# Attention tail on the full tensor array, one more batch of u transposed by DMA, and a new order of work

## The chip, the cores and the metric

The kernel runs on one NeuronCore of a Trainium2 chip. The metric is the time of one execution on the device in microseconds. Five runs of the kernel before gave 216.16 to 217.98 us, with a median of 216.56 us. One execution was recorded by the hardware profiler; all durations below come from it.

The core has a tensor engine (PE), which multiplies matrices into PSUM and loads its stationary operand by separate instructions (PEld); a vector engine (DVE), a scalar engine (ACT) and a general engine (POOL); and SP, whose queue here issues most DMAs. Each engine takes its instructions in the order in which the program gives them, and waits on semaphores for the others.

## The reference

```python
# q, k, v: (8, 8, 576, 64); batch, heads, sequence, head size
kv  = np.einsum('bhsd,bhse->bhde', k, v)
out = np.einsum('bhsd,bhde->bhse', q, kv)
rms = np.sqrt(np.mean(out * out, axis=-1, keepdims=True) + 1e-06)
x   = out / rms * g_norm                     # heads joined: (8, 576, 512)

theta = x @ w_theta
zr, zi = x * np.cos(theta), x * np.sin(theta)
y = einsum('ts,bsd->btd', w_tok_r, zr) + einsum('ts,bsd->btd', w_tok_i, zi)
u = x + y
result = u + np.maximum(u @ w_ch, 0.0)       # float32
```

## The kernel before

**Tiling.** Each of the 8 batches has 576 rows: four full tiles of 128 rows (`NF` = 4, `P` = 128) and a tail of 64 (`T` = 64), five tiles in all (`NT`). The 512 channels are four pairs of heads (`HP` = 4), each of 128 channels. A tail is kept on all 128 partitions: its 64 rows stand there twice, so that the later stages can work on one half of the channels (or on sine and cosine) in each half of the partitions.

**Stages of a batch.** SP loads k, v and q. PE forms kv by head pair (`attention`, L641; tile kv), and ACT or DVE copy it as a block diagonal into `kv_bd` in half precision. q is cast (`qcast`) and transposed to `qT`, whose columns are rows of q: for batches 0 to 3 on PE (`turn_q_pair`, and `turn_q_tail` for the tail), for batches from `Q_DMA` = 4 on by two DMA transposes on SP's queue (`turn_q`, L625 and L631). `norm` (L678) makes raw = q times kv (PE, four matmuls for a full tile), its squares sq (ACT), their sums ss (DVE), the inverse root rt (POOL; ACT and DVE in batch 0) and x = raw times rt (DVE). `turn_x` transposes x on PE (xTps) and ACT copies it to xT with the gain. `phase` makes th = x w_theta (PE), then pt (ACT), f and fa (DVE), two Sin into tr (ACT) and z = x times sine and cosine (DVE). `mix` multiplies z by the turned mixers wT, nine matmuls for a sum y (PE), and DVE adds xT to make uT. `channel` multiplies uT by w_ch (PE, vps), and DVE finishes ot = max(vps, 0) + u, which SP stores.

**u in row order.** `channel` needs u itself, not turned. In batches 0 to 2 and in the last, PE transposes uT (ups, L1116) and ACT copies the outcome to u (L1132). In batches 3 to 6 (`U_FROM` = 3) the four full tiles are made by four DMA transposes on SP's queue instead (ub, L1154), one per 128 channels; the tail is still transposed by PE. There is one buffer for ub.

**The tail of raw.** For the tail, `qT` has 64 columns as the stationary operand, so each matmul fills half of the array's columns (the profile writes the form as 128*64). Two matmuls per head pair, one to each half of the partitions, make the two copies:

```python
for hp in range(HP):
    qT = st["qT", b][:, ti, hp, 0:P if ti < NF else T]
    for rows in (slice(0, P),) if ti < NF else (slice(0, T), slice(T, P)):
        nc.tensor.matmul(
            t[rows, hp * P:(hp + 1) * P], qT, kv_bd[b % 2][:, hp, :],
            start=(hp == 0), stop=(hp == HP - 1),
        )
```

The same half-wide form serves kv, and the tails of th, vps and ups.

**What sets the order.** Nothing is ordered by hand. Every piece of work is a task given to a planner (`Weave`): its name, the engines that can do it with a cost for each, a due time, its needs, and the buffers that it takes and frees. The due time is `START + PERIOD * b + first + every * i`, with (first, every) by stage from the table `DUE`. The planner walks through the tasks with its own clock and fixes the order of each engine's instructions, which engine does a copy, and when a buffer is used again. `SLACK`, `MARGIN`, `AHEAD`, `HOLD`, `DRAIN` and `ENTRY` weigh waits and changes of the array's form against due times. Where PE would have nothing to do before `WARM`, it is given idle work (`warm`, L394). So a change of one constant can move instructions on every engine. The time itself is the hardware's.

Of the kernel before, what the change touches and what calls it, by code (L numbers as in the profile page):

```python
# [15 lines left out]

PERIOD = 26.77
START = 4.0  # L20
DUE = {
    "load": (-21.61, 8.44),
    "theta": (0.63, 0),
    "mixers": (12.92, 0),
    "wch": (22.42, 1.25),
    "wT": (21.7, 1.67),
    ("phase", 0): (19.67, 0),
    ("mix", 0): (28.68, 4.96),
    ("channel", 0): (31.53, 7.53),
    ("phase", 1): (11.06, 3.64),  # L30
    ("mix", 1): (31.8, 5.24),
    ("channel", 1): (50.99, 10.37),
    ("first", 1): (-22.57, 1.61),
    "first": (0.46, 0),
    "cast": (27.66, 0.92),
    "turn_q": (-15.49, 0.49),
    "attention": (-2.51, 1.53),
    "norm": (-0.29, 4.11),
    "turn": (3.55, 1.73),
    "phase": (18.31, 3.76),  # L40
    "mix": (52.82, 3.62),
    "channel": (75.2, 4.08),
}
SLOTS = {
# [5 lines left out]
BANK = {"th": "mm", "y": "mm", "vp": "mm", "pu": "tp", "px": "tp"}  # L50
QUAD = 2
Q_DMA = 4
U_FROM = 3
X_FROM = 8
MIX_AFTER = 2
WCH_AFTER = 8
Q_SOFT = 0
QL_SOFT = 1

# [45 lines left out]
class Weave:  # L105
# [6 lines left out]


    SLACK = {"PE": 0.2, "ACT": 0.004, "DVE": 0.078, "POOL": 0.1, "SP": 0.05}
    MARGIN = {"PE": 0.247, "ACT": 0, "DVE": 0.537, "POOL": 0.1, "SP": 0.0}
    BEGIN = {"PE": 1.6, "ACT": 3.2, "DVE": 1.7, "POOL": 2.5, "SP": 0.73}
    WARM = 71.2
    COLD = 5.0
    URGENT = 5.5
    AHEAD = 0.27  # L120
    HOLD = 2.54
    DRAIN = 0.095
    ENTRY = {"F": 0.011, "R": 0.011, "H": 0.024, "K": 0.048, "Q": 0.048}
    ARRAY = {"F": 0, "R": 1, "H": 2, "K": 2, "Q": 3}
# [137 lines left out]
def kernel(  # L262
# [13 lines left out]
    nc = tc.nc  # L276
    B, H, S, D = q.shape
    C = H * D
    P = 128
    NF = S // P  # L280
    SF = NF * P
    T = S - SF
    NT = NF + 1
    SX = NT * P
    NK = C // P
    HP = H // 2
# [11 lines left out]
    weave = Weave(SLOTS)  # L298
# [6 lines left out]
    def ps(kind, shape, dtype, name):  # L305
        return psum.tile(shape, dtype, tag=kind, bufs=SLOTS[kind], name=name)
# [12 lines left out]
    kv_bd = []  # L319
    for i in range(2):  # L320
        t = const.tile([P, HP, P], FP16, tag=f"kvbd{i}", name=f"kvbd{i}")
# [11 lines left out]
    for i in range(2):  # L333
        t = const.tile([P, NT, H, D], FP16, tag=f"qcast{i}", name=f"qcast{i}")
        nc.gpsimd.memset(t[T:P, NF], 0.0)
        qcast.append(t)
    tails = []
    for i in range(2):
        kl = const.tile([P, H, D], FP32, tag=f"kl{i}", name=f"kl{i}")
        vl = const.tile([P, H, D], FP32, tag=f"vl{i}", name=f"vl{i}")  # L340
# [8 lines left out]
    wch = wpool.tile([P, NK, C], FP16, tag="wch", name="wch")  # L349
# [7 lines left out]
    st = {}  # L357

    def act(n, operands=0, small=False):
        cost = 0.1 + n / 1200.0 + 0.09 * operands  # L360
        return ("ACT", cost, cost + 0.14, False)

    def dve(cost, fast=False):
        return ("DVE", cost, cost + 0.14, fast)

    def pe(cost, form="F"):
        return ("PE", cost, cost + 0.22, form)

    def pool(n):
        return ("POOL", 0.12 + n / 1000.0, 0.17 + n / 1000.0, True)  # L370
# [269 lines left out]
                  uses=[f"qc{b}", f"qT{b}"], dma=dma(0.8))  # L640

    def attention(b, hp):
        def fn(e):
            if hp == 0:
                st["kv", b] = ps("kv", [P, HP, D], FP32, f"kv{b}")
            kvp = st["kv", b]
            for j in range(NT if b >= QUAD else NS):
                for r in range(2):
                    if b < QUAD:
                        half = slice(r * PH, (r + 1) * PH)  # L650
                        (kt, vt) = (st[kind, b, hp][half, j, :] for kind in "kv")
                    else:
                        (kt, vt) = (st[kind, b, hp][:, r, j, :] if j < NF
                                    else st[kind + "l", b][:, 2 * hp + r, :] for kind in "kv")
                    nc.tensor.matmul(  # L655
                        kvp[r * D:(r + 1) * D, hp, :], kt, vt,
                        start=(j == 0), stop=(j == (NT if b >= QUAD else NS) - 1),
                    )

        def keep(e):  # L660
            for r in range(2):
                src = st["kv", b][r * D:(r + 1) * D]
                dst = kv_bd[b % 2][r * D:(r + 1) * D, :, r * D:(r + 1) * D]
                if e == "ACT":
                    nc.scalar.copy(out=dst, in_=src)
                else:
                    nc.vector.tensor_copy(dst, src)

        weave.add(("kv", b, hp), [pe(0.58, "K") if b >= QUAD else pe(1.05, "Q")], due("attention" if b > 1 else "first", b, hp), fn,
                  needs=[("k", b, hp), ("v", b, hp)] + ([("kl", b), ("vl", b)] if b >= QUAD else []),  # L670
                  makes=[] if hp else [("kv", f"kv{b}")],
                  uses=[f"k{b}_{hp}", f"v{b}_{hp}"] + ([f"tails{b}"] if b >= QUAD else []) + ([f"kv{b}"] if hp else []))
        if b > 1 and hp == HP - 1:
            weave.add(("bd", b), [("ACT", 0.65, 0.8, False)], due("attention", b, hp) + 0.1, keep,
                      needs=[("kv", b, i) for i in range(HP)],
                      makes=[("bd", f"bd{b}")], uses=[f"kv{b}"])

    def norm(b, ti):  # L678
        raw, sq, ss, rt, x = (f"{n}{b}_{ti}" for n in ("raw", "sq", "ss", "rt", "x"))
        bank = "raw"  # L680
        at = due("norm", b, ti) if b > 1 else due("first", b, HP)

        def product(e):
            t = st[raw] = ps(bank, [P, C], FP32, raw)
            for hp in range(HP):
                qT = st["qT", b][:, ti, hp, 0:P if ti < NF else T]
                for rows in (slice(0, P),) if ti < NF else (slice(0, T), slice(T, P)):
                    nc.tensor.matmul(  # L688
                        t[rows, hp * P:(hp + 1) * P], qT, kv_bd[b % 2][:, hp, :],
                        start=(hp == 0), stop=(hp == HP - 1),  # L690
                    )

        def square(e):
            t = st[sq] = sb("sq", [P, C], FP32, sq)
            nc.scalar.activation(out=t[:], in_=st[raw][:], func=AFT.Square)  # L695

        def total(e):
            t = st[ss] = sb("ss", [P, H], FP32, ss)
            nc.vector.reduce_sum(  # L699
                out=t[:], in_=st[sq][:].rearrange("p (h e) -> p h e", h=H),  # L700
                axis=mybir.AxisListType.X,
            )

        def root(e):
            t = st[ss]
            nc.gpsimd.tensor_scalar(  # L706
                out=t[:], in0=t[:], scalar1=D * eps, scalar2=None, op0=ALU.add
            )
            r = st[rt] = sb("rt", [P, H], FP32, rt)
            nc.gpsimd.tensor_tensor(out=r[:], in0=t[:], in1=mhalf[:], op=ALU.pow)  # L710

        def root0(e):
            t = st[ss]
            nc.scalar.activation(out=t[:], in_=t[:], func=AFT.Sqrt, bias=eps_t[:])

        def invert0(e):
            r = st[rt] = sb("rt", [P, H], FP32, rt)
            nc.vector.reciprocal(r[:], st[ss][:])

        def scale(e):  # L720
            t = st[x] = sb("x", [P, C], FP16, x)
            nc.vector.tensor_tensor(  # L722
                out=t[:].rearrange("p (h e) -> p h e", h=H),
                in0=st[raw][:].rearrange("p (h e) -> p h e", h=H),
                in1=st[rt][:].unsqueeze(2).broadcast_to((P, H, D)),
                op=ALU.mult,
            )

        qTs = [("qT", b, i) for i in range(NT if b < Q_DMA else 2)]
        bds = [("bd", b)] if b > 1 else [("bd", b, hp) for hp in range(HP)]  # L730
        weave.add((raw,), [pe(0.226, "F" if ti < NF else "H")], at, product, needs=qTs + bds,
                  makes=[(bank, raw)], uses=[f"qT{b}", f"bd{b}"])
        weave.add((sq,), [act(C)], at, square, needs=[(raw,)], makes=[("sq", sq)], uses=[raw])
        weave.add((ss,), [dve(0.59)], at, total, needs=[(sq,)], makes=[("ss", ss)], uses=[sq])
        if b == 0:
            weave.add(("rt0", HP), [("ACT", 0.2, 0.35, False)], at, root0, needs=[(ss,)], uses=[ss])
            weave.add((rt,), [dve(0.12)], at, invert0, needs=[("rt0", HP)], makes=[("rt", rt)],
                      uses=[ss])
        else:
            weave.add((rt,), [("POOL", 2.0, 2.1, False)], at, root, needs=[(ss,)], makes=[("rt", rt)],  # L740
                      uses=[ss])
        weave.add((x,), [dve(0.6)], at, scale, needs=[(rt,)], makes=[("x", x)], uses=[raw, rt])
# [357 lines left out]
    def channel(b, ti):  # L1100
# [5 lines left out]

        pu_on = not U_FROM <= b < B - 1 or ti == NF

# [71 lines left out]
    def due(stage, b, i):  # L1180
        (first, every) = DUE.get((stage, b), DUE[stage])
        return START + PERIOD * b + first + every * i

# [59 lines left out]
```

## Time and profile before

| | us |
|---|---|
| median of five runs | 216.56 |
| the profiled execution, on the device | 217.98 |
| its span, first to last instruction | 216.2 |
| PE busy in the span | 204.2 |
| DVE busy | 178.0 |
| ACT busy | 150.0 |
| POOL busy | 86.5 |
| y on PE (L1067), 576 matmuls | 77.9 |
| th and vps of full tiles on PE (L971, L1125), 128 matmuls each | 31.7 each |
| raw of full tiles (L688), 96 matmuls | 8.6 |
| raw of tails (L688), 64 half-wide matmuls | 3.3 |
| ups of full tiles (L1116), 64 matmuls | 5.9 |
| u copies of full tiles on ACT (L1132), 16 | 9.1 |
| rt on POOL (L710), 31 | 53.9 |

Busy time of an engine is the time covered by its instructions. Consecutive matmuls overlap in the pipeline, so their durations sum to more than the time that they take one after another, and a busy PE can still be held up. The span is what the profiler saw; the time on the device has about 1.8 us around it. The granted clock of PE was full in every slice of the page. DMA moved 45.10 MB at 209 GB/s over the span, with the DMA engines busy most of the time until about 140 us and much less after it.

### The profile page before, as it was taken

What the parts mean: (1) busy time and instruction counts of PE and PEld (TensorE: products, weight loads), DVE (VectorE), ACT (ScalarE), POOL (GpSimd) and SP (SyncE); (2) the same over time, 40 slices, a digit from 0 to 9 for tenths busy, and PEclk for the clock granted to TensorE, in tenths of its full rate; (3) what the DMA queues carried; (4) which work ended last, traced back from release to release, by engine and by line L of the source; (5) the groups of instructions that cost most, each with busy time, mean ns of one, the idle gap of its engine ahead of it and who ended that gap; (6) DMA issues with size and microseconds to landing.
All of it is one profiled execution on the core that took longest, in us unless ns stands there. A gap on an engine that the chain in (4) does not pass through costs nothing.

```text
span 216.2 us, 5949 instructions
## 1 busy us (share of the span) xinstructions
PE 204.2 (94%) x2358; PEld 144.5 (67%) x2358; DVE 178.0 (82%) x357; ACT 150.0 (69%) x291; POOL 86.5 (40%) x101
## 2 busy tenths in 40 slices
PE   6799699999999999999999999999999999999992
PEld 4675377875768667867767677757685667577560
DVE  3295699778988999899999997999898999874652
ACT  2275599977894699978789877968697786740041
POOL 8040104874006740874286348525553645000000
PEclk9999999999999999999999999999999999999999
DMA  6999599999598599997999999784732251345524
GB/s 197 386 353 249 129 341 317 332 295 204 172 291 264 107 307 303 207 290 187 267 206 270 273 248 138 203 292 170 180 85 75 100 121 27 125 136 59 194 80 162
DMA packets 60287, 45.10 MB, mean 209 GB/s; under 512 B 31204, under 2 KB 53348, under 8 KB 60260
## 3 DMA queue, kind: packets, MB, share of 16 engines
q1 hardware_dynamic: 56096, 42.48, 69.8%
q0 software_dynamic: 4160, 2.25, 10.1%
q8 instruction: 18, 0.29, 0.6%
q14 instruction: 9, 0.07, 0.1%
q10 hardware_dynamic: 4, 0.00, 0.0%
HBM read 33.06 MB, written 9.44 MB: 197 GB/s over the span
## 4 chain that ended last, share of the span: by engine, by line
PE 57%; DVE 17%; DMA 12%; POOL 4%; issue 3%; SPq 3%; ACT 2%; DVEq 0%; ACTq 0%
PE y L1067 23%; PE vps L1125 11%; PE th L971 7%; DMA ql<-in_q_dram 6%; PE kv L655 6%; DMA v<-in_v_dram 5%; DVE f L987 3%; PE raw L688 3%; DVE ot L1136 3%; POOL rt L710 3%; PE xTps L918 2%; DVE uT L1078 2%; PE ups L1116 2%; DVE z L1024 2%; SPq L414 2%
## 5 line engine op out<-in xcount | busy, mean ns | idle before, releaser
L1067 PE MATMUL y<-wT,z 128*128 128x320 f16 (+1 forms) x576 | 77.9, 286 | 0.3 <-DVE ot L1136 0.3
L1067 PEld LDWEIGHTS <-z 128*128 128x128 f16 x576 | 54.5, 98 | 16.6 <-issue 2.1
L710 POOL TENSOR_TENSOR rt<-ss,mhalf 128x8 f32<-128x8 f32 x31 | 53.9, 1739 | 2.6
L706 POOL TENSOR_SCALAR ss<-ss 128x8 f32<-128x8 f32 x31 | 9.7, 314 | 67.0 <-DVE ss L699 66.4
L1125 PE MATMUL vps<-wch,uT 128*128 128x512 f16 (+1 forms) x192 | 36.5, 344 | 0.0
L1078 DVE SCALAR_TENSOR_TENSOR uT<-y,gcol,xT 128x320 f16<-128x320 f32 (+1 forms) x48 | 29.1, 612 | 6.3 <-PE y L1067 6.1
L983 ACT ACTIVATE pt<-th,magic_t 128x512 f32<-128x512 f32 (+1 forms) x40 | 25.6, 643 | 11.2 <-PE th L971 10.6
L971 PE MATMUL th<-wth,xT 128*128 128x512 f16 x128 | 31.7, 379 | 0.3 <-DVE f L987 0.2
L655 PE MATMUL kv<-v,k 128*64 128x64 f32 (+1 forms) x672 | 25.4, 222 | 1.5 <-DMA v<-in_v_dram 1.2
L987 DVE SCALAR_TENSOR_TENSOR f<-pt,th 128x512 f32<-128x512 f32 (+1 forms) x40 | 24.8, 626 | 2.1 <-ACT pt L983 2.1
L655 PEld LDWEIGHTS kv<-v,k 128*64 128x64 f32 (+1 forms) x672 | 22.6, 137 | 4.6 <-issue 2.7
L927 ACT ACTIVATE xT<-xTps,gcol 128x512 f16<-128x512 f16 (+1 forms) x32 | 20.1, 629 | 7.7 <-PE xTps L918 7.4
L1132 ACT COPY u<-ups 128x512 f16<-128x512 f16 (+1 forms) x24 | 12.1, 513 | 17.5 <-PE ups L1116 17.4
L1006 ACT ACTIVATE tr<-fa,pio_t 128x512 f16<-128x512 f32 x32 | 22.8, 719 | 2.0 <-DVE fa L994 1.9
L722 DVE TENSOR_TENSOR x<-raw,rt 128x512 f16<-128x512 f32 x32 | 21.9, 685 | 2.4 <-POOL rt L710 2.2
L699 DVE TENSOR_REDUCE ss<-sq 128x8 f32<-128x512 f32 x32 | 21.7, 679 | 2.1 <-ACT sq L695 1.7
L1006 ACT ACTIVATE tr<-f 128x512 f16<-128x512 f32 x32 | 20.0, 630 | 4.9 <-DVE f L987 4.7
L1125 PEld LDWEIGHTS <-uT 128*128 128x128 f16 (+1 forms) x192 | 14.8, 102 | 10.8 <-issue 0.5
L1024 DVE TENSOR_TENSOR z<-x,tr 128x1024 f16<-128x1024 f16 (+1 forms) x32 | 19.7, 619 | 1.1 <-ACT tr L1014 0.8
L971 PEld LDWEIGHTS <-xT 128*128 128x128 f16 x128 | 11.9, 98 | 11.7 <-ACT xT L927 0.9
L695 ACT ACTIVATE sq<-raw 128x512 f32<-128x512 f32 x32 | 18.8, 591 | 0.8 <-PE raw L688 0.8
L599 DVE CAST qcast<-q 128x512 f16<-128x512 f32 x32 | 13.4, 420 | 5.1 <-DMA q<-in_q_dram 5.1
(101 smaller groups left out, 261.9 us busy)
## 6 DMA issues: line engine op xcount, KB each, us to landing
q<-in_q_dram SPq DMA_DIRECT2D x32, 256.0 KB, 5.2
out_dram<-ot SPq DMA_DIRECT2D x32, 256.0 KB, 2.7
k<-in_k_dram SPq DMA_DIRECT2D x24, 256.0 KB, 5.2
v<-in_v_dram SPq DMA_DIRECT2D x24, 256.0 KB, 5.4
k<-in_k_dram SPq DMA_DIRECT2D x8, 288.0 KB, 5.6
v<-in_v_dram SPq DMA_DIRECT2D x8, 288.0 KB, 5.7
wst<-in_moe_w_theta_dram SPq DMA_DIRECT2D x4, 256.0 KB, 7.3
out_dram<-ot SPq DMA_DIRECT2D x16, 64.0 KB, 2.1
```

What stands on the lines that cost most here:

```text
L655: nc.tensor.matmul(kvp[r * D:(r + 1) * D, hp, :], kt, vt, start=(j == 0), stop=(j == (NT if b >= QUAD else NS) - 1),)
L699: nc.vector.reduce_sum(out=t[:], in_=st[sq][:].rearrange("p (h e) -> p h e", h=H), axis=mybir.AxisListType.X,)
L710: nc.gpsimd.tensor_tensor(out=r[:], in0=t[:], in1=mhalf[:], op=ALU.pow)
L722: nc.vector.tensor_tensor(out=t[:].rearrange("p (h e) -> p h e", h=H), in0=st[raw][:].rearrange("p (h e) -> p h e", h=H), in1=st[rt][:].un ...
L971: nc.tensor.matmul(t[:], xT[:, kc, :], wth[:, kc, :], start=(kc == 0), stop=(kc == NK - 1),)
L983: nc.scalar.activation(out=t[:], in_=st[th][:], func=AFT.Identity, bias=magic_t[:])
L987: nc.vector.scalar_tensor_tensor(out=t[:], in0=st[pt][:], scalar=MAGIC, in1=st[th][:], op0=ALU.subtract, op1=ALU.subtract,)
L1006: nc.scalar.activation(out=t[:, which, :], in_=src[:], func=AFT.Sin, scale=-RAD, bias=0.0 if bias is None else bias[:],)
L1024: nc.vector.tensor_tensor(out=t[:], in0=xb.unsqueeze(1).broadcast_to((P, w, C)), in1=st[tr][:, 0:w, :], op=ALU.mult,)
L1067: nc.tensor.matmul(st[y][:, c, :], z[:, kc * P:(kc + 1) * P], wT[m][:, cols], start=(c == 0 and m == 0) if open_sums else m == 0, stop=m = ...
L1078: nc.vector.scalar_tensor_tensor(out=st["uT", b][:, chunks, cols], in0=st[y][:], scalar=gcol[:], in1=st["xT", b][:, chunks, cols], op0=ALU ...
L1125: nc.tensor.matmul(t[half], uT(kc), wch[:, kc, r * n:(r + 1) * n], start=(kc == 0), stop=(kc == NK - 1),)
```

## The change

Three things change, and the constants of the planner with them.

1. The tail's 64 columns of `qT` are copied beside themselves (task `qTd`, on ACT, DVE or POOL as the planner chooses), so that the stationary operand has 128 columns, and raw of a tail is made by the same four full matmuls as a full tile. A full tile now needs only the full columns of `qT`; the tail needs the copy.
2. `U_FROM` goes from 3 to 2: the full tiles of u of batch 2 are made by four DMA transposes instead of 16 PE transposes and four ACT copies.
3. The due times and weights of the planner are new, so the order is planned anew on every engine. `attention` can now take several head pairs as one task (`KV_RUN`), but with `KV_RUN = 1` it takes one, as before.

```diff
-PERIOD = 26.77
+PERIOD = 26.95
...
-    "theta": (0.63, 0),
-    "mixers": (12.92, 0),
-    "wch": (22.42, 1.25),
+    "theta": (0.39, 0),
+    "mixers": (17.6, 0),
+    "wch": (24.7, 1.25),
...
-    ("mix", 1): (31.8, 5.24),
-    ("channel", 1): (50.99, 10.37),
-    ("first", 1): (-22.57, 1.61),
+    ("mix", 1): (31.68, 5.24),
+    ("channel", 1): (50.99, 7.88),
+    ("first", 1): (-24.56, 1.26),
...
-    "norm": (-0.29, 4.11),
-    "turn": (3.55, 1.73),
+    "norm": (-1.15, 4.11),
+    "turn": (4.17, 1.73),
...
-    "mix": (52.82, 3.62),
-    "channel": (75.2, 4.08),
+    "mix": (51.46, 2.87),
+    "channel": (75.2, 4.3),
...
-U_FROM = 3
+U_FROM = 2
...
-    MARGIN = {"PE": 0.247, "ACT": 0, "DVE": 0.537, "POOL": 0.1, "SP": 0.0}
+    MARGIN = {"PE": 0.247, "ACT": 0.026, "DVE": 0.555, "POOL": 0.1, "SP": 0.0}
...
-    WARM = 71.2
+    WARM = 69.7
...
-    AHEAD = 0.27
-    HOLD = 2.54
+    AHEAD = 0.3
+    HOLD = 2.45
...
             for hp in range(HP):
-                qT = st["qT", b][:, ti, hp, 0:P if ti < NF else T]
-                for rows in (slice(0, P),) if ti < NF else (slice(0, T), slice(T, P)):
-                    nc.tensor.matmul(
-                        t[rows, hp * P:(hp + 1) * P], qT, kv_bd[b % 2][:, hp, :],
-                        start=(hp == 0), stop=(hp == HP - 1),
-                    )
+                nc.tensor.matmul(
+                    t[:, hp * P:(hp + 1) * P], st["qT", b][:, ti, hp, :], kv_bd[b % 2][:, hp, :],
+                    start=(hp == 0), stop=(hp == HP - 1),
+                )
...
-        qTs = [("qT", b, i) for i in range(NT if b < Q_DMA else 2)]
+        qTs = [("qT", b, i) for i in range(HP)] if b < Q_DMA else [("qT", b, 0)]
+        if ti == NF:
+            qTs.append(("qTd", b))
+
+            def double(e):
+                (out, src) = (st["qT", b][:, NF, :, r * T:(r + 1) * T] for r in (1, 0))
+                if e == "ACT":
+                    nc.scalar.copy(out=out, in_=src)
+                elif e == "DVE":
+                    nc.vector.tensor_copy(out, src)
+                else:
+                    nc.gpsimd.tensor_copy(out, src)
+
+            weave.add(("qTd", b), [act(HP * T), dve(0.2, True), pool(HP * T)], at - 1.0, double,
+                      needs=[("qT", b, HP if b < Q_DMA else 1)], uses=[f"qT{b}"])
...
-        weave.add((raw,), [pe(0.226, "F" if ti < NF else "H")], at, product, needs=qTs + bds,
+        weave.add((raw,), [pe(0.226)], at, product, needs=qTs + bds,
                   makes=[(bank, raw)], uses=[f"qT{b}", f"bd{b}"])
```

In the planned order this gives 5 doubling copies on ACT and 3 on POOL, 32 full matmuls for raw of the tails instead of 64 half-wide ones, 16 ups matmuls fewer, four DMA transposes more on SP's queue, and 50 pieces of idle work on PE instead of 55.

More of the change, by code (lines that the diff above doesn't have):

```diff
@@ L56 @@
 WCH_AFTER = 8
+KV_RUN = 1
 Q_SOFT = 0
@@ L642, in attention, with times @@
     def attention(b, hp):
+        run = KV_RUN if b >= QUAD and b > 1 else 1
         def fn(e):
-            if hp == 0:
+            if hp == run - 1:
                 st["kv", b] = ps("kv", [P, HP, D], FP32, f"kv{b}")
+            for i in range(hp - run + 1, hp + 1):
+                times(i)
+        def times(hp):
             kvp = st["kv", b]
@@ L667, in keep @@
                     nc.vector.tensor_copy(dst, src)
[L669 to L672, printed above, removed]
+        if hp % run == run - 1:
+            pairs = range(hp - run + 1, hp + 1)
+            kvn = [("kv", f"kv{b}")]
+            weave.add(("kv", b, hp), [pe(0.58 * run, "K") if b >= QUAD else pe(1.05, "Q")],
+                      due("attention" if b > 1 else "first", b, hp), fn,
+                      needs=[(kind, b, i) for kind in "kv" for i in pairs]
+                      + ([("kl", b), ("vl", b)] if b >= QUAD else []),
+                      makes=kvn if hp == run - 1 else [],
+                      uses=[f"{kind}{b}_{i}" for kind in "kv" for i in pairs]
+                      + ([f"tails{b}"] if b >= QUAD else []) + ([] if hp == run - 1 else [f"kv{b}"]))
         if b > 1 and hp == HP - 1:
             weave.add(("bd", b), [("ACT", 0.65, 0.8, False)], due("attention", b, hp) + 0.1, keep,
-                      needs=[("kv", b, i) for i in range(HP)],
+                      needs=[("kv", b, i) for i in range(run - 1, HP, run)],
                       makes=[("bd", f"bd{b}")], uses=[f"kv{b}"])
```

## The prediction

> **What bounds the kernel now.** I read first the page's totals and its row of 40 slices, then busy time by stretches of 20 us, then the order of time on the tensor engine (PE).
>
> ```profile
> PE 204.2 (94%) x2358; PEld 144.5 (67%) x2358; DVE 178.0 (82%) x357; ACT 150.0 (69%) x291; POOL 86.5 (40%) x101
> PE   6799699999999999999999999999999999999992
> PE 57%; DVE 17%; DMA 12%; POOL 4%; issue 3%; SPq 3%; ACT 2%; DVEq 0%; ACTq 0%
> ...
> 80.00:100.00 20.00, 20.00 (x288) 15.03 (x286) 18.88 (x37) 18.12 (x36) 9.94 (x11) 1.00 1.06 255
> 100.00:120.00 20.00, 20.00 (x223) 14.29 (x222) 19.15 (x39) 16.77 (x33) 10.30 (x10) 1.00 0.98 240
> 120.00:140.00 20.00, 19.87 (x245) 14.88 (x244) 18.67 (x37) 15.79 (x31) 11.58 (x13) 1.00 1.22 213
> 140.00:160.00 20.00, 20.00 (x235) 14.14 (x234) 18.87 (x38) 15.02 (x28) 9.45 (x9) 1.00 0.68 195
> ```
>
> The columns of the stretches are the span, then PE, weight loads, DVE, ACT and POOL. From 80 to 160 us PE has no gap and DVE is busy 75.6 of 80. But a busy PE may still be waiting inside a pipelined matmul, so what counts is the distance from one start to the next:
>
> ```profile
> 75.20 0.39 PE L918 MATMUL xTps<-ident,x 128*128 128x128 f16 x4
> 75.52 0.41 PE L688 MATMUL raw<-kvbd,qT 128*64 128x128 f16 x8
> 75.77 0.63 PE L655 MATMUL kv<-v,k 128*64 128x64 f32 x16
> 76.24 0.28 PE L655 MATMUL kv<-vl,kl 128*64 128x64 f32 x4
> 76.35 0.34 PE L655 MATMUL kv<-v,k 128*64 128x64 f32 x6
> ...
> 110.22 0.40 PE L918 MATMUL xTps<-ident,x 128*128 128x128 f16 x4
> 110.45 0.39 PE L688 MATMUL raw<-kvbd,qT 128*128 128x128 f16 x4
> 110.68 0.39 PE L1116 MATMUL ups<-ident,uT 128*128 128x128 f16 x4
> 110.90 0.38 PE L1125 MATMUL vps<-wch,uT 128*128 128x512 f16 x1
> ```
>
> Each row is one group: start, duration, tile written, array form. Groups of one kind have the same distance to their successor nearly everywhere after 62 us: four 128x128 pieces 0.23, four of 128x512 0.86, nine of 128x320 1.22. The few longer ones in the rows to 190 us add up to about 1.8 us of real waiting. **So from 62 us to the end the sum of PE's pieces sets the time**, and DVE is close behind. Loads are not near: between the landing of a batch's last k or v and its first use lie 5 us or more from batch 2 on.
>
> **Part 1, the tail's product.** It goes from eight pieces in the half-wide form (128*64) to four full ones. The rows price it: 75.52 to 75.77 is 0.25; 110.45 to 110.68 is 0.23, and 0.22 elsewhere. Eight batches by 0.03: **−0.24**. What speaks against the change is a rule of the Trainium skill: TensorEngine Tiling (Array Packing), Overview, gives up to twice the speed for a stationary operand of at most 64 columns, packed in tiles. But here both halves compute the same rows twice, so two packed pieces do what one doubled piece does, and the row shows no gain left to lose: read as a factor of two lost the rule would give +0.25 per batch, +2.0 in all; the row gives −0.24, and I take the row.
>
> The same page (Tiling Modes, Key Properties) says that a change of tiling mode drains the engine. The row agrees and gives the size: xTps takes 0.32 before the half-wide product and 0.23 before a full one, so 0.10 per change of form. If every tail shed its two changes, that would be 16 x 0.10 = 1.6 us. I counted the changes in both orders instead: 61 before, 57 after, because the tail mostly stood beside kv pieces, which are half-wide too, and keep their own changes. **−0.40.** I take the count.
>
> **Part 2, the doubling copies.** Eight of 128x256 f16: five on ACT, three on POOL. No row shows this one; the nearest are ACT's u copy of 128x256 (372 ns, L1132) and POOL's copy into wtt of 128x256 (399 ns, L528). So ACT +1.9, POOL +1.2. From below a copy can't cost less than nothing; from above it delays the raw of the tail by about 0.4 + 0.3 of handover, eight times. The cover: the transposed q's tail lands long before use (batch 4 at 100.1 us against its raw at 116.2, batch 5 at 121.3 against 136.8), and in the new order full tiles no longer wait for the tail's columns. On POOL only rt and ss are queued behind it, and POOL is 40% busy; on ACT, Sin and Square wait 0.37. I take 0 of PE's time, up to 0.8 if the cover on ACT is gone in some batches.
>
> **Part 3, u of batch 2.** Off PE: 4 groups of four transposes, 4 x 0.22 = **−0.88**. Off ACT: 4 x 0.584 (L1132) = −2.3. Added: four DMA transposes issued by SP, each 1.24 us of SP's queue, 2.5 us to landing in the quiet stretches and up to 4.8 in the crowded one. They go between the loads of batch 6 and the q transposes of batch 5, so SP's queue shifts by 5 us; behind it are k and v of batch 6, which landed 10.6 to 19.6 us before use. The finishing adds of batch 2 (DVE, in order) wait for the landing: from the last y of batch 2 to its first product with w_ch the new order has about 15 us of PE pieces at the rows' prices, against 11 for the adding of uT (0.55), the issue of a q transpose that stands before the last one (4.3, L625), its own 1.24 and 4.8 to landing. No cost at PE; if that cover failed, DVE would stop us for us.
>
> **Part 4, the new order.** The other gap it can close stands at 61 us, where PE has nothing ready while ACT copies kv of batch 2 (L665):
>
> ```profile
> 61.12 0.73 ACT L665 CAST kvbd<-kv 64x256 f16<-64x256 f32 x2
> 61.24 0.27 PE L394 MATMUL warm<-kvbd 128*128 128x256 f16 x1
> 61.35 0.28 PE L891 MATMUL qTpl<-ident,qcast 128*128 128x64 f16 x4
> 61.47 0.38 PE L394 MATMUL warm<-kvbd 128*128 128x256 f16 x2
> 62.15 0.38 PE L688 MATMUL raw<-kvbd,qT 128*128 128x128 f16 x4
> ...
> 64.29 0.45 DVE L1024 TENSOR_TENSOR z<-x,tr 128x512 f16<-128x512 f16 x1
> 64.77 0.49 PE L1067 MATMUL y<-wT,z 128*128 128x256 f16 x3
> ```
>
> The idle-work pieces (warm) fill 0.11 + 0.68 = 0.79 us. In the new order ups and vps of batch 0 stand there, and one idle piece follows later: 0.79 − 0.11 = **−0.68**. But the last rows show a second thin place. y of a batch can't start before z of its tail, which comes from th of the tail through pt, f, fa, two Sin and z. In the old order batch 1's z ended at 64.74 and y began at 64.77, with nothing to spare. Chain from th's start to z's end, against the PE pieces between th's start and y in the new order, priced by the rows: batch 1 6.66 against 5.96; batch 3 6.66 against 6.36; batch 7 4.72 against 4.30; the others are covered by 1 us or more. If the chains stay as long, PE waits 0.70 + 0.30 + 0.42 = 1.42. They may shorten (in batch 7 f waited 0.7 for DVE), so between 0 and 1.4: I take half, **+0.7**, since in the old order a chain could be slow unpunished. The sum over the other small waits I leave as it is, ±1 us. Before 40 us nearly all instructions keep their places: 0, ±0.4.
>
> **Sum:** −0.24 − 0.40 − 0.88 − 0.68 + 0.7 = −1.5. The profiled execution took 217.98 (span 216.2 and 1.8 around it) and would take 216.5; the median shown, 216.56, is 1.4 below the profiled one, and I carry the difference over: **215.1**, own range 213.8 to 216.2.
>
> **Rivals.**
>
> *Forecast: faster by PE's sum (0.54).* For it: the even distances between starts. Time 215.1.
>
> *No change: DVE takes over (0.23).* DVE has only 4.4 us free between 80 and 160 and gives back little: its list of copies loses some 0.8 us (three more of about 0.4 to 0.45, six fewer, at the rows' durations), nearly all in the first 75. If DVE holds the pace from 62 to 160, what PE saves there (0.88 of u, 5 x 0.03 of tails, about 0.3 of form changes: 1.3) comes back as waits, and 0.2 is left: 216.4. Against it: PE shows no waits there, so DVE runs ahead.
>
> *Slower: the tail's chain is uncovered (0.23).* Place: the head of each batch's y, in batches 1, 3 and 7 first. Price: the full shortfall is 1.42; each us by which ACT or DVE stretch a chain (copies put in, another order of f, x, ot) adds up to 1 us per such batch. Savings without waits are 2.2, so it decides from 2.2 + 1.1 = 3.3 us of new waits, that is chains longer by 0.6 us in three batches. At 1 us longer: 1.42 + 3.0 − 2.2 = +2.2, or 218.8; at 0.7, 217.9. For it: fillers became thinner in exactly these batches while DVE is nearly full; against it: ACT has lost 2.3 us at batch 2, and the chains had slack in the old order except at batch 1.
>
> That the change doesn't do what it says is excluded for parts 1 to 3: in the new order 64 half-wide pieces have become 32 full ones, 16 transposing matmuls are gone and four DMA transposes have come.
>
> **Numbers.** A measurement of this kernel can tell about 0.5% (1.1 us) from no change: faster is below 215.5, slower above 217.6. The forecast's own spread puts about 0.52 below 215.5 with a little from better orders; the second case and the forecast's upper end give 0.25; the third 0.23. The range goes from 213.3 (no shortfall, other waits 1 less) to 218.0 (third case at 0.7).
>
> **What would show it.** Right: rows of raw with x4 in the full form for tails, 0.22 apart; no ups of batch 2; starts as even as now after 62 us; no idle pieces near 61; y of batch 1 starting within 0.5 us after the pieces before it. Wrong: waits of PE's y for DVE's z of the tail in batches 1, 3 or 7; waits of DVE's ot for the DMA ub; waits of ACT for the landing of qT's tail; DVE at 20.0 of 20 in the stretches with PE waiting for it.

## The result, and the profile after

The changed kernel takes 214.56 us (median of 24 runs, 213.75 to 217.62) against 216.51 us for the kernel before (45 runs): a ratio of 0.9914, 95% interval 0.9898 to 0.9930, or 1.9 us less. Medians are of all runs; ratios leave out the few runs in a slower state. The forecast was 215.1, with a range of 213.3 to 218.0. The profiled execution of after took 216.28 us with a span of 214.5; that of before 217.98 with 216.2. They lie 1.7 and 1.5 above their medians, so the two spans may be compared.

First the page of after: totals, and the shares of the chain that ended last.

```profile
PE 203.8 (95%) x2305; PEld 144.9 (68%) x2305; DVE 177.2 (83%) x355; ACT 150.6 (70%) x294; POOL 89.0 (41%) x104
PE 58%; DMA 15%; DVE 8%; ACT 7%; POOL 6%; issue 2%; SPq 2%; DVEq 0%
```

PE has 53 matmuls fewer and DVE, ACT and POOL have nearly the same work. In the chain, DVE's share fell from 17% to 8%, and DMA's rose from 12% to 15%. Next the stretches of 20 us (span, PE, weight loads, DVE, ACT, POOL, then granted clock and DMA):

```profile
80.00:100.00 20.00, 19.77 (x252) 14.21 (x247) 19.57 (x41) 18.83 (x39) 10.14 (x11) 1.00 1.06 254
100.00:120.00 20.00, 20.00 (x235) 15.05 (x233) 19.46 (x39) 17.23 (x32) 11.63 (x13) 1.00 0.87 203
120.00:140.00 20.00, 20.00 (x237) 14.64 (x235) 18.96 (x37) 15.00 (x30) 10.14 (x10) 1.00 0.95 240
140.00:160.00 20.00, 20.00 (x229) 13.44 (x226) 19.89 (x39) 16.28 (x32) 12.95 (x12) 1.00 0.76 220
```

PE is still full, but DVE now works 77.9 of these 80 us, where it worked 75.6 before. Its total hardly changed (177.2 for 178.0), but more of it falls into this stretch, and 2.1 us are left free.

To see where the time went I took the distance from each group's start on PE to the next start, and subtracted the price that the same pieces have where nothing holds them up. What is left is idle work, waits and changes of form:

| us | before | after |
|---|---|---|
| pieces at their undisturbed price | 181.5 | 180.4 |
| rest, before 40 us | 18.9 | 18.4 |
| rest, 40 to 70 us | 2.6 | 3.0 |
| rest, 70 to 190 us | 6.6 | 6.4 |
| rest, from 190 us | 0.8 | 0.8 |

The pieces' own sum gives 1.1 of the 1.5 that this account shows, as parts 1 and 3 said; the other 0.2 between the spans lies behind PE's last piece. The 0.5 before 40 us says nothing, since executions of one order stand up to 2.5 us apart there (last section). The rest hides gains and losses that nearly cancel, and they are in the rows in order of time. The tail's product of batch 2, in the full form, among its neighbours:

```profile
76.14 0.39 PE L943 MATMUL xTps<-ident,x 128*128 128x128 f16 x4
76.36 0.39 PE L699 MATMUL raw<-kvbd,qT 128*128 128x128 f16 x4
76.58 0.39 PE L1141 MATMUL ups<-ident,uT 128*128 128x128 f16 x4
```

Starts are 0.22 apart, as forecast. At 61 us the idle pieces are gone. One stands at the head of y of batch 1:

```profile
65.75 0.28 PE L395 MATMUL warm<-kvbd 128*128 128x256 f16 x1
66.09 4.09 PE L1092 MATMUL y<-wT,z 128*128 128x256 f16 x36
```

Elsewhere such a piece takes 0.11 to the next start (61.24 to 61.35 in before). Here it takes 0.34: y starts just behind its end, at 65.75 + 0.28 = 66.03. This looks like the wait for z of the tail that the prediction named, at half its size, for DVE makes that z at about the same time (square brackets give the engine's idle time before the row, and what ended it):

```profile
65.57 0.43 DVE L1049 TENSOR_TENSOR z<-x,tr 128x512 f16<-128x512 f16 x1 [0.22 <-ACT tr L1039]
```

It ends at 66.00. But it is not that wait. In `d2_dve_more` (below) DVE is a little later against PE; the distance is 0.34 again, and y starts 0.11 before z has ended:

```profile
65.25 0.28 PE L395 MATMUL warm<-kvbd 128*128 128x256 f16 x1
65.59 4.09 PE L1093 MATMUL y<-wT,z 128*128 128x256 f16 x36
```

```profile
65.27 0.43 DVE L1050 TENSOR_TENSOR z<-x,tr 128x512 f16<-128x512 f16 x1 [0.23 <-ACT tr L1040]
```

In all eight profiles of kernels with after's order here, the distance is 0.33 or 0.34. And in after, y of batch 2 starts at 93.99 (rows below), when z of its tail is only being begun:

```profile
94.00 0.42 DVE L1049 TENSOR_TENSOR z<-x,tr 128x512 f16<-128x512 f16 x1 [0.43 <-ACT tr L1039]
```

In batch 3, y starts at 111.62 and z of the tail ends at 111.80; neither y is held up. The kernel says why: a sum y is nine matmuls, and only the ninth (`m == 2 * NF`) reads z of the tail. At 0.11 each, that is 0.87 us after y's start, and in every batch from 1 on z was ready by then, in after with 0.4 us or more to spare. So the 0.34 is the price of the idle piece itself.

In batch 7 the prediction named a shortfall of 0.42, and there is none. y follows the pieces before it at once:

```profile
192.32 0.68 PE L1150 MATMUL vps<-wch,uT 128*64 128x256 f16 x8
192.93 4.24 PE L1092 MATMUL y<-wT,z 128*128 128x256 f16 x37
```

Two waits are new and had not been named. In the first, PE stops for DVE's x behind y of batch 2:

```profile
93.99 2.13 PE L1092 MATMUL y<-wT,z 128*128 128x256 f16 x18
96.35 0.40 PE L943 MATMUL xTps<-ident,x 128*128 128x128 f16 x4 [0.23 <-DVE x L733]
```

From 93.99 to 96.35 are 2.36 us for eighteen pieces that take 1.97 elsewhere. DVE had itself waited 0.43 for the Sin in front of z of the tail (row at 94.00), and x is the fourth piece behind that z in its queue. So the tail's chain probably does cost time here, through DVE's order and not through y; no run separates this. The second is the larger one. The first product with w_ch stops in the middle for its weights:

```profile
54.51 0.60 PE L1150 MATMUL vps<-wch,uT 128*128 128x512 f16 x2
55.80 0.59 PE L1150 MATMUL vps<-wch,uT 128*128 128x512 f16 x2 [0.69 <-DMA wch<-in_moe_w_ch_dram]
56.23 0.39 PE L783 MATMUL qTps2h<-ident,qcast 128*128 128x128 f16 x4
```

From 54.51 to 56.23 are 1.72 us for a group that takes 0.86. POOL's queue in the same execution shows why:

```profile
43.85 1.68 POOL L855 TENSOR_TENSOR rt1h<-ss1h,mhalf 128x8 f32<-128x8 f32 x1
45.50 1.51 POOL L544 DMA_DIRECT2D wch<-in_moe_w_ch_dram  x2
```

Its two fetches stand behind one more root task than before. The new due time of w_ch (24.7 for 22.42) is not what put them there: with the old due times and the edits (`c1_old_constants`, below) they stand behind the same third root and are issued at 44.8, and with the new due times alone (`c2_constants_alone`) they stand in front of it and are issued at 40.8. So they moved with the edits, by way of the planner. They were issued at 41.7 and 42.4 before and are issued at 45.5 and 46.3 now; their landing takes 8.2 to 9.5 us, and PE wants the second 8.6 us after its issue.

### The profile page after: what moved, and what is told of

It is laid out like the page before. It is cut to its first block, busy times and chain, and to the rows that moved or that the text cites. A ratio compares the mean times of both kernels' runs of the same rounds, so it can differ in the third digit from the quotient of the medians.

```text
span 214.5 us, 5833 instructions
## 1 busy us (share of the span) xinstructions
PE 203.8 (95%) x2305; PEld 144.9 (68%) x2305; DVE 177.2 (83%) x355; ACT 150.6 (70%) x294; POOL 89.0 (41%) x104
## 4 chain that ended last, share of the span: by engine, by line
PE 58%; DMA 15%; DVE 8%; ACT 7%; POOL 6%; issue 2%; SPq 2%; DVEq 0%
PE y L1092 25%; PE vps L1150 12%; PE th L996 8%; DMA ql<-in_q_dram 6%; PE kv L662 5%; DMA wch<-in_moe_w_ch_dram 4%; POOL rt L721 3%; DMA v<-in_v_dram 3%; PE raw L699 2%; PE xTps L943 2%; POOL rt1h L855 2%; ACT tr L1031 2%; DMA k<-in_k_dram 2%; PE ups L1141 2%; DVE x L733 2%
## 5 line engine op out<-in xcount | busy, mean ns | idle before, releaser
L721 POOL TENSOR_TENSOR rt<-ss,mhalf 128x8 f32<-128x8 f32 x31 | 55.8, 1801 | 2.6
L717 POOL TENSOR_SCALAR ss<-ss 128x8 f32<-128x8 f32 x31 | 8.4, 272 | 56.6 <-DVE ss L710 55.9
L662 PE MATMUL kv<-v,k 128*64 128x64 f32 (+1 forms) x672 | 27.0, 233 | 0.0
L662 PEld LDWEIGHTS kv<-v,k 128*64 128x64 f32 (+1 forms) x672 | 24.2, 146 | 3.7 <-issue 3.1
L1157 ACT COPY u<-ups 128x512 f16<-128x512 f16 (+1 forms) x20 | 9.9, 500 | 16.8 <-PE ups L1141 16.8
```

Source lines behind the costliest of these rows:

```text
L662: nc.tensor.matmul(kvp[r * D:(r + 1) * D, hp, :], kt, vt, start=(j == 0), stop=(j == (NT if b >= QUAD else NS) - 1),)
```

## The experiments

Twelve more kernels ran, each 5 to 22 times, with the kernel before beside it. Ratios are to before; differences between kernels are taken between ratios, times 216.5 us, since the median of before moved from 216.5 to 216.8 between sets.

**Undoing one part in the new order.** In these the planned order of everything else is exactly that of after.

`a1_half_wide`: the tail's product half-wide again, without the copies.

```diff
-                nc.tensor.matmul(
-                    t[:, hp * P:(hp + 1) * P], st["qT", b][:, ti, hp, :], kv_bd[b % 2][:, hp, :],
+                qT = st["qT", b][:, ti, hp, 0:P if ti < NF else T]
+                for rows in (slice(0, P),) if ti < NF else (slice(0, T), slice(T, P)):
+                    nc.tensor.matmul(
+                        t[rows, hp * P:(hp + 1) * P], qT, kv_bd[b % 2][:, hp, :],
...
```

> The order of the changed kernel, but raw of each tail again from eight half-wide matmuls, and no doubling copies. By the sum of PE's pieces: 8 x 0.03 for the pieces, and the changes of the array's form rise from 57 to 71, 14 x 0.10, together +1.6 us: 216.2 against 214.6 of the changed kernel. If DVE sets the pace: 0 to +0.3, 214.6 to 214.9. If the copies cost time where they stand: less than +1.6 by what they cost.

Measured: 215.51, ratio 0.9951 (0.9933 to 0.9970), so 0.8 us above after. The same tail of batch 2 here:

```profile
73.81 0.39 PE L947 MATMUL xTps<-ident,x 128*128 128x128 f16 x4
74.12 0.41 PE L701 MATMUL raw<-kvbd,qT 128*64 128x128 f16 x8
74.47 0.40 PE L1145 MATMUL ups<-ident,uT 128*128 128x128 f16 x4
```

The distances are 0.31 and 0.35, where after has 0.22 and 0.22: two changes of form and eight pieces cost 0.22 more. That holds for the tails of batches 2, 4, 5 and 6; in batch 3 a wait of 0.1 hides part of it, and in batch 7 the tail follows a half-wide vps, and raw and its neighbours take 2.52 us in both. The sum over batches 2 to 7 is 1.0. The expected 1.6 counted all eight tails at full price, the first two of which lie in the front.

`a4_half_copies`: the same, with the copies kept.

```diff
 half-wide product as in a1_half_wide; the task qTd copies as in after
```

> The order of after with the half-wide tail again and the doubling copies kept, though nothing reads what they write. Against a1_half_wide (215.5), which differs by the copies alone, the copies cost nothing if the work beside them hides them: 215.5. If they delay ACT or POOL, up to the 0.8 that the prediction allowed: 216.3.

Measured: 215.68, ratio 0.9970 (0.9939 to 1.0000). That is 0.4 us above a1, with intervals that overlap. In the profile the distance between the two grows by 0.2 us from 27 us to the end, and 0.14 of this is a longer wait for w_ch at 53 us. The copies are hidden, or nearly so.

`a2_u_by_pe`: u of batch 2 by PE and ACT again, in front of its products with w_ch, and its four DMA transposes left out.

```diff
+            if b == 2 and ti < NF:
+                turn(e)
+                nc.scalar.copy(out=st["ub", b][:, ti, :], in_=st[pu][:])
             t = st[vp] = ps(BANK["vp"], [P, n], FP32, vp)
...
```

> The order of the changed kernel, but u of batch 2 again from PE transposes and ACT copies, each put just ahead of the tile's product with w_ch; its four DMA transposes left out. By the sum of PE's pieces: 4 x 0.22 = +0.9 us, 215.5; a little more if the four ACT copies (2.3 us) delay a Sin that PE waits for. If DVE sets the pace: +0 to +0.2.

Measured: 215.25, ratio 0.9951 (0.9928 to 0.9975), 0.8 above after. In its order of time each ups takes the place that it was priced at:

```profile
120.08 0.39 PE L1141 MATMUL ups<-ident,uT 128*128 128x128 f16 x4
120.30 1.03 PE L1153 MATMUL vps<-wch,uT 128*128 128x512 f16 x4
121.17 0.39 PE L1141 MATMUL ups<-ident,uT 128*128 128x128 f16 x4
```

Four times 0.22 is lost there and nowhere else. Part 3's price stands.

`a3_wch_early`: the two fetches of w_ch, and the hold in front of them, moved up in POOL's queue before the second of its root tasks of batch 1; nothing else moves.

```diff
...
+        early = [x for x in log if x[0] in ("hold_ch", ("wch", 0), ("wch", 1))]
+        log = [x for x in log if x not in early]
+        at = [x[0] for x in log].index(("rt1h1",))
+        for (_, e, fn) in log[:at] + early + log[at:]:
+            fn(e)
```

> The order of the changed kernel, but the two fetches of w_ch stand earlier in POOL's queue, before the second root of batch 1, so that the first product with w_ch no longer waits for them (0.69 us in the trace of the changed kernel). If this wait stands on the path: -0.7 us, 213.9. If the next thing of the start-up is late anyway: -0.2 to 0, 214.4 to 214.6.

Measured: 213.27, ratio 0.9863 (0.9837 to 0.9888), below after's whole interval. This version beats both kernels. PE at the same place:

```profile
52.16 1.03 PE L1155 MATMUL vps<-wch,uT 128*128 128x512 f16 x4
53.02 0.39 PE L788 MATMUL qTps2h<-ident,qcast 128*128 128x128 f16 x4
```

The group takes 0.86 again. Its fetches are issued at 35.8 and 36.6. Against the profile of after it gains 0.86 us here and nothing behind it. In the six other kernels here that keep after's order up to this place the group took 0, 0.03, 0.44, 0.49, 0.63 and 0.97 us more than 0.86, and in after 0.86 more: it depends on when the fetch lands, and is 0.5 in the mean. The gain of 1.1 us in the ratios is more than that. `a5_y_behind`, which leaves the fetches alone, stands 1.0 below after too, so part of the 1.1 may have nothing to do with them; what it is isn't settled.

`a5_y_behind`: the fourth sum y of batch 7 put back behind the fourth vps of batch 6, as before had it (the reason is below).

```diff
-vps6_2, y7_3, vps6_3 (PE)    ot6_2, uT7_3, ot6_3 (DVE)
+vps6_2, vps6_3, y7_3 (PE)    ot6_2, ot6_3, uT7_3 (DVE)
```

> The order of after with the fourth sum y of batch 7 put back behind the fourth vps of batch 6, and its adding behind the fourth ot, as in the order of before. If the new sequence at the end is part of the gain, the wait for a store comes back: 215.1 to 216.0. If the end has slack in this order as it has in that of before: 214.6.

Measured: 214.26, ratio 0.9866 (0.9819 to 0.9913), 1.0 below after, with intervals that overlap. No loss that can be told: the place at the end is worth nothing in this order.

**Doing one part in the old order.** `b1_tail_only`: before's order, with the tail's product on the full array; the engine that writes the tail's columns writes them twice (batches 0 to 3), or ACT copies them ahead of the batch's first raw.

```diff
+            if ti == 0 and b >= Q_DMA:
+                (to, half) = (st["qT", b][:, NF, :, r * T:(r + 1) * T] for r in (1, 0))
+                nc.scalar.copy(out=to, in_=half)
...
```

> The order of the kernel before, with raw of the tails from four full matmuls and the doubled columns written by the engine that writes the tail's columns (batches 0 to 3) or by an ACT copy at the batch's first raw (4 to 7). Changes of form fall from 61 to 55. By the sum of PE's pieces: -0.24 - 0.6 = -0.8 us, 215.7. If the gain is all the new order's: 216.5. If DVE sets the pace: 216.4.

Measured: 218.42, ratio 1.0092 (1.0062 to 1.0122): a miss, slower than before. DVE near the end, and PE after it:

```profile
200.21 0.69 DVE L1138 SCALAR_TENSOR_TENSOR ot<-vps,ub 128x512 f32<-128x512 f32 x1 [0.17 <-PE vps L1127]
203.67 0.69 DVE L1138 SCALAR_TENSOR_TENSOR ot<-vps,ub 128x512 f32<-128x512 f32 x1 [2.77 <-DMA out_dram<-ot]
```

```profile
202.32 0.60 PE L1127 MATMUL vps<-wch,uT 128*64 128x256 f16 x8
204.41 1.79 PE L1069 MATMUL y<-wT,z 128*128 128x320 f16 x12 [1.48 <-DVE ot L1138]
```

There are three buffers for ot. The fourth ot of batch 6 waits for the store of the first, DVE waits with it, and PE's y waits for the buffer that DVE would free. In before's profile DVE's wait for the store is 0.54.

`b2_tail_y_ahead`: b1, with y of batch 7 and its adding put in front of that fourth vps.

```diff
...
+        ahead = [x for x in log if x[0] in (("y7_3", 4), ("uT", 7, 3))]
+        log = [x for x in log if x not in ahead]
+        at = [x[0] for x in log].index(("vps6_3",))
+        for (_, e, fn) in log[:at] + ahead + log[at:]:
+            fn(e)
```

> The order of before with the full-array tail, as in b1_tail_only (218.4), and the fourth sum y of batch 7, with its adding to uT on DVE, put ahead of the fourth vps of batch 6, as the new order has it. If b1 lost its gain at the end, where DVE's fourth ot of batch 6 waited 2.8 us for the store of the first and PE's y waited for DVE, that wait is covered now: 216.0 to 216.9, and no wait of y for ot above 0.5 us after 200 us. If b1 lost it to the copies or to the order in the middle, nothing changes: 218.4.

Measured: 217.02, ratio 1.0029 (1.0004 to 1.0054), 1.4 us below b1 and still not below before. So b1 lost most of its time at the end, but the tail's gain isn't there either. Its rows of batch 2 answer to those of before at 75.20:

```profile
76.25 0.39 PE L925 MATMUL xTps<-ident,x 128*128 128x128 f16 x4
76.47 0.39 PE L694 MATMUL raw<-kvbd,qT 128*128 128x128 f16 x4
76.79 0.69 PE L660 MATMUL kv<-v,k 128*64 128x64 f32 x16
77.31 0.29 PE L660 MATMUL kv<-vl,kl 128*64 128x64 f32 x4
```

Before: 0.32 + 0.25 + 0.47 = 1.04 for xTps, raw and the first kv. Here: 0.22 + 0.32 + 0.52 = 1.06. The change of form has moved from in front of raw to behind it, and kv takes 0.05 more. It is so in batches 2, 4, 5 and 6 (batch 3 alike, with a half-wide ups behind). Only batch 7, with no kv behind, saves 0.23. In its profile b2 stands 1.04 us behind before at 56 us and 0.93 at the end, so the 0.6 by which its ratio is worse doesn't arise behind 56 us in this execution. About half of it can be placed ahead of that. In b1 and b2 the cast that writes the tail's columns is made twice on DVE, one behind the other:

```profile
52.47 0.75 DVE L908 CAST qT<-qTpl 128x256 f16<-128x256 f32 x2
```

It took 0.41 in before. The f behind it comes 0.33 later, ACT waits 0.19 for f, and between about 49 and 56 us PE falls back by 0.33 to 0.34 in both kernels, where b3, the same order with the old tail, keeps its distance. So these doubled copies, unlike those of after, are probably not hidden; where the other half stands is open.

`b3_y_ahead`: before with that move at the end alone.

```diff
 order of before; y7_3 and uT7_3 ahead of vps6_3, as in b2_tail_y_ahead
```

> Before, with only the fourth sum y of batch 7 and its adding put ahead of the fourth vps of batch 6. If the place at the end costs before what its profile shows (0.5 us): 216.1. If the store of the first ot of batch 6 takes 4.3 us instead of 2.1 in many executions, up to 1.5 less: 215.1. If that place is nothing: 216.6.

Measured: 216.64, ratio 1.0006 (0.9983 to 1.0030): nothing. With a5, the end has slack in both orders, and the store came late in b1.

**Edits and constants apart, each planned anew.** `c1_old_constants` has both edits and before's constants; `c2_constants_alone` has the new constants without the edits.

```diff
 c1: after, with PERIOD, DUE, MARGIN, WARM, AHEAD and HOLD of before
 c2: before, with PERIOD, DUE, MARGIN, WARM, AHEAD and HOLD of after
```

> Both edits (full-array tail with its copies, u of batch 2 by DMA), planned anew with the constants of before. 65 changes of the array's form against 61 before and 57 after, and at the end the old sequence with y behind the fourth vps of batch 6. Sum of PE's pieces: -0.24 - 0.88 + 4 x 0.06 to 0.10 = -0.8, so 215.8, and 216 to 217.5 if the end waits for a store as in b1. If the edits alone carry the gain: 214.6.

> The new constants without the edits: half-wide tail, u of batch 2 by PE. 85 changes of form against 61, and the new sequence at the end. Sum of PE's pieces: 24 x 0.06 to 0.10 = +1.4 to +2.4, end -0.5 to -1: 217.0 to 218.5. If the new constants alone carry the gain: 214.6.

Measured: c1 219.16, ratio 1.0117 (1.0076 to 1.0158); c2 221.30, ratio 1.0195 (1.0148 to 1.0243). Neither half carries the gain, and both came out 1.7 and 2.8 us above the upper ends that were expected. In c1, PE stands still where it was full in before and after (first row: stretches; second: PE in order of time):

```profile
80.00:100.00 20.00, 18.96 (x263) 13.52 (x260) 18.15 (x36) 17.86 (x36) 10.67 (x11) 1.00 0.92 229
```

```profile
95.95 1.02 PE L996 MATMUL th<-wth,xT 128*128 128x512 f16 x4 [0.63 <-DVE ot L1161]
```

PE waits for a buffer that DVE's ot frees, and DVE is idle 1.85 of these 20 us, among others in waits for sq (0.77) and rt (0.34) between two of its ot. With the old constants the edits cost 2.5 us; with the new ones they gain 6.1 (from c2 to after). What they are worth is set by the order around them.

**More work on one engine.** `d1_pe_more` does each xTps of a full tile twice (batches 2 to 7); `d2_dve_more` does fa of two full tiles per batch twice (batches 1 to 7). Both write the same values again.

```diff
-            for kc in range(NK):
+            for kc in list(range(NK)) * (2 if ti < NF else 1):
```

```diff
+            for _ in range(2 if b and ti in (0, 2) else 1):
                 nc.vector.tensor_scalar(
```

> The order of after with each of the 24 groups of xTps of full tiles (batches 2 to 7) done twice: 24 x 0.22 = 5.3 us more of PE's pieces. If PE's sum sets the time from 62 us on: +5.3, so 219.8. If DVE sets the pace, the pieces fall into PE's waits: 214.6 to 215.6.

> The order of after with fa of two full tiles in each of batches 1 to 7 done twice: 14 x about 0.34 = 4.8 us more on DVE. DVE is free for 2.1 of the 80 us from 80 to 160, and 2.7 of the 4.8 fall there. If PE's sum sets the time, the free time takes most of it: 214.6 to 215.6. If DVE sets the pace: up to +4.8, so 219.4.

Measured: d1 219.48, ratio 1.0115 (1.0077 to 1.0154), +4.4 us over after for 24 x 0.22 = 5.3 us of pieces. d2 218.35, ratio 1.0059 (1.0026 to 1.0091), +3.1 us. What d2 added was more than expected. DVE's own rows:

```profile
102.58 0.88 DVE L1020 TENSOR_SCALAR fa<-f 128x512 int32<-128x512 int32 x2
103.37 0.68 DVE L710 TENSOR_REDUCE ss<-sq 128x8 f32<-128x512 f32 x1
...
106.42 0.42 DVE L1020 TENSOR_SCALAR fa<-f 128x512 int32<-128x512 int32 x1
106.75 0.69 DVE L733 TENSOR_TENSOR x<-raw,rt 128x512 f16<-128x512 f32 x1
```

A pair takes 0.79 to the next start and a single 0.33, so each repeat costs about 0.46 and all fourteen about 6.4 us, where 0.34 and 4.8 were expected. About half of it reaches the end. PE then waits where it had not, or for longer:

```profile
93.78 2.12 PE L1093 MATMUL y<-wT,z 128*128 128x256 f16 x18
96.53 0.40 PE L943 MATMUL xTps<-ident,x 128*128 128x128 f16 x4 [0.62 <-DVE x L733]
```

This wait was 0.23 in after. Added work on PE comes through at 0.8 of its length, on DVE at 0.5: PE's sum sets the time first, but DVE has almost no cover left.

## Why the prediction was right, step by step

**PE's sum from 62 us on** holds: d1 pays for 4.4 of 5.3 us, and a1 and a2, which put the old pieces back, lose 0.8 us each. Together that is 1.6 of the 1.9 gained. It was stated too strongly: d2 shows that the rival with DVE is at work in part, and the wait for x in batch 2 is a place where it already shows.

**Part 1.** The price of a change of form, 0.10, and of the pieces, 0.03, is what a1's rows show. The edit is worth 0.8 us by the ratios and 1.0 by the rows in the new order and, by b2's rows, next to nothing in the old one beside kv. The term of −0.40 for 61 to 57 changes was mis-sized by place: five fewer fall between 40 and 70 us, but from 70 to 190 us the new order has 34 where the old had 32.

**Part 2.** Taken at 0, with 0.8 as its upper end; 0.4 by the ratios, not told from 0, and less than 0.1 in the profiles without the wait for w_ch. The copies of b1 and b2, placed otherwise, probably cost 0.3.

**Part 3.** −0.88 taken, 0.8 by the ratio and four times 0.22 in a2's rows. No wait of ot for ub appears at batch 2.

**Part 4.** The idle work at 61 us went, as taken, but the one piece left, priced at 0.11, took 0.34: −0.45 in place of −0.68. The shortfall of +0.7 rested on a step that is wrong, that y of a batch can't start before z of its tail. Only the ninth matmul of a sum needs that z, and y started 0.43 and 0.18 us before it was ready in batches 2 and 3 without waiting. In before, y of batch 1 began 0.03 behind it, which was chance, not a wait. So the shortfall is 0, and the 0.34 that falls within 0 to 0.7 is the idle piece. What also failed is the claim that other places stay as they are. Its step "before 40 us nearly all instructions keep their places" stopped short of 45 us, where w_ch had gone behind a root in POOL's queue: 0 to 0.97 us of waiting, the largest single item that the order added. On the other side, the old order's waits went: groups from 70 us on that were longer than their undisturbed price by more than 0.15 us had 1.7 us of it before and have 0.9 now, 0.4 of which is the new wait for x. The allowance of 1 us either way held these. That the sum of −1.5 came near the measured −1.9 is in part luck, for a term without ground (+0.7) stood against waits that had not been seen.

**The rivals.** The uncovered chain did not decide: no head of y waits for z of the tail, and the chain shows at most in the 0.4 for x in batch 2. DVE taking over did not either, but its margin is as thin as the rival said.

## What to carry to other kernels

In these rows a change of the array's form is paid at the border between two forms (about 0.10 us), so an edit that removes a narrow piece is worth its changes only where both neighbours are wide; look at the neighbours in the order that will run. When a planner makes the order, the edit and its constants can't be priced apart: walk through every queue of the new order, also those that only issue fetches, and ask of each moved fetch when it lands and who needs it. When a late tile feeds a group of instructions, look up which of them reads it: the group can start ahead of it. With two engines near full, measure the slope of both by adding work before calling one of them the bound.

## What the hardware showed unexpectedly

Doing fa twice in a row into the same tile takes 0.79 us where one takes 0.33: the second starts 0.45 to 0.46 behind the first in thirteen of fourteen pairs, just after its end (0.42), where another instruction starts 0.33 behind it. No run shows why. The store of an ot kept its buffer for about 2.3 us after the ot was made in before (the ot that ended at 200.53 let the fourth start at 202.80), and for 4.5 us in b1 (199.17 to 203.67), at a time when little else moved (26 GB/s from 195 to 200 us); no run shows why. And with the same order of instructions, profiled executions stand up to 2.5 us apart by 27 us (a5 against after) and carry that distance on, so a difference of 1 us between two single profiles says nothing about two kernels unless the place where it arises is shown.
